# Sliding-window attention with a gated MLP: VectorE precedence for product additions in the last three blocks, in place of a hold on the second projection product in blocks 2 to 5

## Chip, cores and metric

One core of one Trainium2 chip. The metric is device time of one execution in microseconds, the median over the runs; a profiled execution gives the trace. Engines are named as in the profile: PE is TensorE, DVE is VectorE, ACT is ScalarE, POOL is GpSimd, SP is SyncE.

## What is computed

The reference runs causal attention with a window of 128 positions and an ALiBi bias (8 batches, 8 heads, 576 positions, head size 64), and passes the result through a gated MLP:

```python
scores = scale * q @ k.T;  bias = -slope[h] * |i - j|;  mask = 0 <= i - j < 128
x = softmax(where(mask, scores + bias, -1e9)) @ v         # then (4608, 512)
g = x @ w_gate                                             # w_gate, w_val: 512 x 1536
out = (g * sigmoid(g) * (x @ w_val)) @ w_out               # w_out: 1536 x 512
```

Inputs and output are 32-bit floats; the kernel computes with 16-bit operands and accumulates in PSUM in 32 bits.

## The kernel before

The 4608 tokens are nine blocks of 512 (n = 0 to 8). For each block the kernel needs x transposed (`xT`), then the hidden activations `hT` (1536 x 512, in 12 row groups m), then the projection with `w_out`. Attention for later tokens runs between the pieces of MLP work of earlier ones, until all attention is done in block 5.

**Gate and value.** In blocks 0 to 5 they are direct products: for each m one *half* is the gate (pg, L400, four matmuls of 512 columns, then tanh L418 on ScalarE and L419 on VectorE), the other the value (pv, L400, then L430 into `hT`). A block has 24 halves, counted from 0. In blocks 6 to 8 (`SEVEN_FROM = 6`) two row groups at a time, a *unit* u of 0 to 5, are computed by the seven-product scheme of Strassen (`gate_val_by_seven`, all matmuls L627): `first`, `fifth`, `second`, `sixth`, `third`, `seventh`, `fourth`. Products pile up in PSUM tiles gX, gY, gZ. VectorE adds after two of them: `third` (v1 = gY + u2, L663, then L664 into `hT`) and `seventh` (v2 = gX + p5, L670). `fourth` writes gX again, so it can't start before L670 has read gX; L679 then multiplies its SiLU by v2 into `hT`.

**Projection.** The projection of a block n >= 1 is also done by seven products (`strassen(n, t)`, matmuls L535), once for each half t of its columns, so 14 parts. Part 0 is A11 B11, part 1 (the *second projection product*) accumulates into the tile p (`p2`), part 2 is S2 T2, then S1 T1, S3 T3, S4 B22, A22 T4. VectorE makes S1 to S4 from `hT` as *sums*, for three groups c of row groups: L488 (S3), L489 (S1, in place), L490 (S2), L491 (S4). `half_plus` (L540) adds two products on VectorE for the output. The tile p2 comes from the pool `ps_a` (four banks, shared with the scores) while the gate and value of the next block are direct, and from `ps_f` afterwards. In blocks 2 to 5 the parts of the block before are spread over the halves: one part after each half whose number is in `AT = {1, 3, 4, 6, 7, 9, 11, 13, 14, 15, 17, 18, 20, 22}`, so the second products are due after halves 3 and 14. In blocks 6 to 8 one part follows every third step. The projection of block 8 is a closing stage of its own, in which both t alternate.

**Attention.** `scores` issues a group of products into `ps_a`: four banks for a wide tile (L280), two for a narrow one (L316); ScalarE takes the exponential (L286, L320) of each bank, VectorE multiplies by the mask (L292, L324). `weighted` gives av (L348).

**Order.** From step 60 on TensorE's order is that of the program text (`manual_schedule` for PE alone). The orders of VectorE and ScalarE are fixed when the program is built, by a planner that steps through its own estimate of time: whenever an engine is free it takes, of the instructions that it holds to be ready, the one that comes first in the program. Instructions issued under `tc.high_priority()` are taken ahead of all others that are ready. On the chip each engine then runs its queue in order. `later` holds sums that `ffn` issues one or two per step.

The hold that the change touches is in `ffn`: `scored[0]` is cleared before each half is handed to the driver, which may then issue attention steps; `products()` sets it. `given` counts the parts issued in the block.

Of the kernel before, what the change touches and what calls it, by code (L numbers as in the profile page):

```python
# [31 lines left out]
SEVEN_FROM = 6  # L32
# [19 lines left out]
def kernel(  # L52
# [10 lines left out]
    nc = tc.nc  # L63
# [175 lines left out]
        nc.sync.dma_start_transpose(transposed_home(name, rank), t_.rearrange("p h d -> p (h d)"))  # L239

    ex = {}
    scored = [False]

    def scores(i):

        s, p = units[i]
        def combined(n):
            return scores_128(s, (3, 7, 8)[n], 8, (s, "c", n), msk[n])

        def together(one, two):  # L250
            return [one[0] + two[0]] + one[1:] + two[1:]

        if p == 8:
            first = combined(0) if s == 0 else []
            return first + together(combined(1), combined(2))
        if p == 7 and s == 0:
            return scores_128(s, p, p, (s, p), reg[:, :, 0:P])
        if p == 7:
            return together(scores_128(s, p, p, (s, p), reg[:, :, 0:P]), combined(0))
        if p == 3:  # L260
            return scores_128(s, p, p, (s, p), reg[:, :, 0:P], i < FIRST)
        ks = (9 * s + p) % NK
        banks = []
        early_tile = i < FIRST
        e = epool.tile([P, H, 256], FP16, name="ex", tag="ex", bufs=4)
        ex[(s, p)] = e

        def products():
            scored[0] = True
            for q4 in range(2):  # L270
                two = [ps_a.tile([P, 2, 256], FP32, name="ps", tag="a") for _ in range(2)]
                banks.append(two)
                for par in range(2 if early_tile else 0):
                    o = 4 * q4 + 2 * par
                    nc.tensor.matmul(two[par], idm, bias[:, o:o + 2, :], start=True, stop=False)
                for j in range(2):
                    pair = 2 * q4 + j
                    for par in range(2):
                        rows = slice(64 * par, 64 * par + 64)
                        nc.tensor.matmul(two[par][:, j, :], kT[rows, ks, pair, :],  # L280
                                         qT[rows, p:p + 2, pair, :], start=(j == 0 and not early_tile),
                                         stop=(j == 1))

        def act(q4, par):
            o = 4 * q4 + 2 * par
            nc.scalar.activation(e[:, o:o + 2, :], banks[q4][par], AF.Exp, scale=scale)  # L286

        def mul(q4):
            if early_tile:
                return  # L290
            o = slice(4 * q4, 4 * q4 + 4)
            nc.vector.tensor_mul(e[:, o, :], e[:, o, :], reg[:, o, :])  # L292

        return [[products], [lambda: act(0, 0)], [lambda: act(0, 1), lambda: mul(0)],
                [lambda: act(1, 0)], [lambda: act(1, 1), lambda: mul(1)]]

    def scores_128(s, kt, qt, key, m, early_tile=False):

        ks = (9 * s + kt) % NK
        banks = []  # L300
        e = epool.tile([P, H, P], FP16, name="exc", tag="exc", bufs=5)
        ex[key] = e

        er4 = e.rearrange("k (a par b) q -> k a par b q", a=2, par=2)

        def products():
            scored[0] = True
            banks.extend(ps_a.tile([P, 4, P], FP32, name="psc", tag="a") for _ in range(2))
            for par in range(2 if early_tile else 0):
                nc.tensor.matmul(banks[par].rearrange("k (a b) q -> k a b q", a=2), idm,  # L310
                                 bias.rearrange("k (a par b) q -> k a par b q", a=2, par=2)
                                 [:, :, par, :, 0:P], start=True, stop=False)
            for j in range(4):
                for par in range(2):
                    rows = slice(64 * par, 64 * par + 64)
                    nc.tensor.matmul(banks[par][:, j, :], kT[rows, ks, j, :], qT[rows, qt, j, :],  # L316
                                     start=(j == 0 and not early_tile), stop=(j == 3))

        def act(par):
            nc.scalar.activation(er4[:, :, par], banks[par].rearrange("k (a b) q -> k a b q", a=2),  # L320
                                 AF.Exp, scale=scale)

        return [[products], [lambda: act(0)],
                [lambda: act(1), lambda: early_tile or nc.vector.tensor_mul(e, e, m)]]  # L324
# [182 lines left out]
    def strassen(n, t):  # L507
# [12 lines left out]
        else:  # L520
            po = ps_f.tile([P, 2, HC], FP32, name="po", tag="po", bufs=1)
            X, Y = po[:, 0, :], po[:, 1, :]
# [13 lines left out]
                                 stop=(m == HM - 1), skip_group_check=True)  # L536

        def half_plus(dst, a, b):
            with tc.high_priority() if n + 1 < SEVEN_FROM else ExitStack():
                nc.vector.scalar_tensor_tensor(out=dst, in0=a, scalar=factor, in1=b,  # L540
                                               op0=ALU.mult, op1=ALU.add)

# [72 lines left out]
    def gate_val_by_seven(n):  # L615

        x = xT[n]
        A11, A12 = x[:, 0:HK, 0:256], x[:, HK:NKB, 0:256]
        S1, A22 = x[:, 0:HK, 256:512], x[:, HK:NKB, 256:512]
        S2, S3, S4 = xsum.pop(n)  # L620
        hT[n] = hpool.tile([P, NMB, 512], FP16, name="hT", tag="hT")
        live = {}

        def product(dst, w, c0, a, start=False):
            for i in range(2):
                for kb in range(HK):
                    nc.tensor.matmul(dst[:, i, :], w[:, kb, c0 + i * P:c0 + (i + 1) * P], a[:, kb, :],  # L627
                                     start=(start and i == 0 and kb == 0),
                                     stop=(i == 1 and kb == HK - 1), skip_group_check=True)

        def first(u):
            X, Y = (ps_a.tile([P, 2, 256], FP32, name=i, tag="a", bufs=4) for i in ("gX", "gY"))
            Z = ps_f.tile([P, 2, 256], FP32, name="gZ", tag="gv")
            live[u] = X, Y, Z
            product(X, G1, 2 * u * P, A11, True)
            nc.scalar.copy(Z, X)

        def fifth(u):
            Y = live[u][1]
            product(Y, tsum[u][0], 0, S1, True)  # L640
            p5 = epool.tile([P, 2, 256], FP32, name="p5", tag="exc", bufs=5)
            nc.scalar.copy(p5, Y)
            live[u] += (p5,)

        def second(u):
            Z = live[u][2]
            product(Z, G2, 2 * u * P, A12)
            s = supool.tile([P, 2, 256], FP16, name="s1", tag="tt")
            nc.scalar.activation(s, Z, AF.Silu)
            live[u] += (s,)  # L650

        def sixth(u):
            X = live[u][0]
            product(X, tsum[u][1], 0, S2)
            u2 = epool.tile([P, 2, 256], FP32, name="u2", tag="exc", bufs=5)
            nc.scalar.copy(u2, X)
            live[u] += (u2,)

        def third(u):
            X, Y, Z, p5, u2, s = live[u][:6]  # L660
            product(Y, V2, 2 * u * P, S4)
            v_ = supool.tile([P, 2, 256], FP16, name="v1", tag="uu")
            nc.vector.tensor_add(v_, Y, u2)  # L663
            nc.vector.tensor_mul(hT[n][:, 2 * u:2 * u + 2, 0:256], s, v_)  # L664

        def seventh(u):
            X, Y, Z, p5, u2, s = live[u]
            product(X, tsum[u][2], 0, S3)
            v_ = supool.tile([P, 2, 256], FP16, name="v2", tag="uu")
            nc.vector.tensor_add(v_, X, p5)  # L670
            live[u] += (v_,)

        def fourth(u):
            X, v_ = live[u][0], live[u][-1]
            del live[u]
            product(X, tsum[u][3], 0, A22)
            s = supool.tile([P, 2, 256], FP16, name="s2", tag="tt")
            nc.scalar.activation(s, X, AF.Silu)  # L678
            nc.vector.tensor_mul(hT[n][:, 2 * u:2 * u + 2, 256:512], s, v_)  # L679

        return {f.__name__: f for f in (first, second, third, fourth, fifth, sixth, seventh)}
# [23 lines left out]
    def ffn():  # L705

        for n in range(NBLK):
# [5 lines left out]
                        yield 1.0  # L713
            if n == SEVEN_FROM:
                break
            due, given = 0, 0
            for m in range(NMB):
                for half, _ in enumerate(gate_val(n, m)):
                    scored[0] = False
                    yield 1.0  # L720
                    due += n > 1 and 2 * m + half in AT
                    while due and not (scored[0] and given % 7 == 1):
                        next(parts)
                        due, given = due - 1, given + 1
                        yield 0.75
                    if n > 1:
                        for _ in range(1 + (len(later) > 3)):
# [285 lines left out]
```

## Time and profile before

| | |
|---|---|
| median of 4 runs | 343.28 us (343.01 to 343.58) |
| profiled execution | 343.34 us, of which 341.6 us are the span of the trace |
| busy: PE, DVE, ACT, POOL | 330.1, 277.4, 207.0, 109.6 us |
| granted TensorE clock, mean over the span | 0.998 |
| chain that ended last, by engine | PE 78%, DVE 13%, ACT 5% |

The stages of the trace, from TensorE's timeline, with the busy time of PE and DVE in each:

| stage | us | PE busy | DVE busy |
|---|---|---|---|
| block 2 and start of 3 | 95.7 to 144.0 | 47.7 | 42.1 |
| blocks 3 and 4 | 144.0 to 208.0 | 64.0 | 59.8 |
| block 5 | 208.0 to 243.4 | 35.4 | 35.3 |
| block 6 and start of 7 | 243.4 to 271.4 | 28.0 | 18.6 |
| block 7 and start of 8 | 271.4 to 299.7 | 27.7 | 20.2 |
| block 8 | 299.7 to 327.5 | 27.5 | 18.6 |
| closing projection, stores | 327.5 to 341.6 | 9.5 | 6.8 |

How to read the trace's lines: a timeline line is the start, the time to the end of the last of a merged run, the engine, the line of the kernel, the operation, output<-inputs with the shape, and how many were merged; in brackets the idle time before it and what ended it. A VectorE instruction's row is longer than its place in the queue: a sum has a row of 0.42 us while the next may start 0.33 us after it, an addition from PSUM of 512 columns a row of 0.69 us and a spacing of 0.60 us. A list of waits gives the engine, line and tile that waited, what it waited for, the total in us, the number of times, and the longest.

### The profile page before, as it was taken

Reading aid. Unit: us, or ns where it says so; the run is one execution under the profiler, and the core shown is the slowest. Engines: PE = TensorE matmul, PEld = TensorE weight load, DVE = VectorE, ACT = ScalarE, POOL = GpSimd, SP = SyncE. Lnnn points to the kernel's source line nnn. Section 1 sums busy time; section 2 is a strip of 40 time slices with the busy share of each in tenths; the row PEclk is TensorE's granted clock in tenths of the full one; section 3 lists DMA queues with packets and bytes.
Section 4 is the critical chain, followed back from the end, with each engine's and each line's share of the span. In section 5 each row is a group of like instructions: output and inputs, shape, how many; then the busy total and the mean of one; then the engine's idle time right before and its main releaser. Section 6 shows DMA issues by size and latency. Waiting matters only on the chain.

```text
span 341.6 us, 7787 instructions
## 1 busy us (share of the span) xinstructions
PE 330.1 (97%) x2983; PEld 218.6 (64%) x2983; DVE 277.4 (81%) x652; ACT 207.0 (61%) x412; POOL 109.6 (32%) x136
## 2 busy tenths in 40 slices
PE   7999989999999999999999999999999999999994
PEld 4484445444456566566655655666788878888884
DVE  6577885999798779998899999999855975765683
ACT  3758676465765675666655557463477667676640
POOL 8968672649675176834017000000000000000000
PEclk9999999999999999999999999999999999999999
DMA  9999999999999999999949922041101101011014
GB/s 151 171 180 175 163 170 154 79 129 160 142 173 156 156 180 169 170 159 149 195 108 98 182 33 79 15 84 26 63 15 48 63 0 64 26 38 63 0 71 116
DMA packets 160037, 37.37 MB, mean 109 GB/s; under 512 B 147328, under 2 KB 155648, under 8 KB 160000
## 3 DMA queue, kind: packets, MB, share of 16 engines
q0 software_dynamic: 118336, 18.62, 81.4%
q1 hardware_dynamic: 40976, 17.64, 29.1%
q10 hardware_dynamic: 688, 0.62, 0.6%
q8 instruction: 23, 0.38, 0.4%
q14 instruction: 14, 0.11, 0.1%
HBM read 37.91 MB, written 9.44 MB: 139 GB/s over the span
## 4 chain that ended last, share of the span: by engine, by line
PE 78%; DVE 13%; ACT 5%; issue 2%; DMA 1%; SPq 0%; DVEq 0%
PE po L535 16%; PE pg L400 15%; PE pv L400 15%; PE gX L627 8%; PE av L348 4%; PE gY L627 4%; PE ps L280 4%; PE po L454 2%; PE p L535 2%; DVE hT L430 2%; PE gZ L627 2%; DVE uu L419 2%; ACT ex L286 2%; PE px L374 1%; ACT tt L418 1%
## 5 line engine op out<-in xcount | busy, mean ns | idle before, releaser
L400 PE MATMUL pv<-xT,wv_sb 128*128 128x512 f16 (+2 forms) x320 | 76.5, 358 | 0.6 <-DVE uu L419 0.3
L400 PE MATMUL pg<-xT,wg_sb 128*128 128x512 f16 (+2 forms) x320 | 75.8, 358 | 0.3 <-DVE xT L376 0.2
L418 ACT ACTIVATE tt<-pg 128x512 f16<-128x512 f32 (+2 forms) x70 | 41.3, 590 | 47.7 <-PE pg L400 46.6
L286 ACT ACTIVATE ex<-ps 128x512 f16<-128x512 f32 x96 | 50.0, 606 | 10.1 <-PE ps L280 10.1
L419 DVE SCALAR_TENSOR_TENSOR uu<-tt,pg 128x512 f16<-128x512 f16 (+2 forms) x69 | 45.9, 665 | 10.5 <-ACT tt L418 10.3
L430 DVE TENSOR_TENSOR hT<-uu,pv 128x512 f16<-128x512 f16 (+2 forms) x70 | 46.6, 665 | 3.0 <-PE pv L400 1.3
L185 POOL DMA_DIRECT2D va<-in_v_dram x40 | 34.4, 865 | 34.5 <-PE av L348 28.8
L400 PEld LDWEIGHTS <-wv_sb 128*128 128x128 f16 x320 | 28.3, 98 | 25.1 <-issue 3.2
L535 PEld LDWEIGHTS <-hT 128*128 128x128 f16 x384 | 37.0, 98 | 10.6 <-issue 0.8
L400 PEld LDWEIGHTS <-wg_sb 128*128 128x128 f16 x320 | 28.2, 98 | 23.3 <-issue 2.2
L191 POOL DMA_DIRECT2D kn<-in_k_dram x39 | 33.3, 857 | 20.7 <-DMA kT<-kn 11.9
L191 POOL DMA_DIRECT2D qn<-in_q_dram x39 | 33.5, 864 | 17.6 <-DMA va<-in_v_dram 9.9
L535 PEld LDWEIGHTS <-S 128*128 128x128 f16 x288 | 27.3, 98 | 8.9 <-issue 1.4
L292 DVE TENSOR_TENSOR ex<-ex,m_reg 128x1024 f16<-128x1024 f16 x42 | 28.7, 685 | 3.1 <-ACT ex L286 3.0
L351 DVE TENSOR_TENSOR x<-av,rec 128x256 f16<-128x256 f32 x72 | 28.8, 419 | 0.4
L535 PE MATMUL po<-T,S 128*128 128x256 f16 x192 | 26.5, 273 | 0.6 <-DVE S L490 0.3
L535 PE MATMUL po<-T,hT 128*128 128x256 f16 x192 | 26.0, 273 | 0.0
L679 DVE TENSOR_TENSOR hT<-s,v 128x512 f16<-128x512 f16 x18 | 7.6, 424 | 18.5 <-ACT s L678 18.5
L320 ACT ACTIVATE exc<-psc 128x512 f16<-128x512 f32 x40 | 21.3, 609 | 1.9 <-PE psc L316 1.9
L348 PEld LDWEIGHTS <-ex 128*128 128x128 f16 x384 | 17.4, 97 | 4.6 <-issue 1.2
L348 PE MATMUL av<-va,ex 128*128 128x65 f16 x384 | 19.3, 193 | 0.7 <-DMA kn<-in_k_dram 0.5
L280 PE MATMUL ps<-qT,kT 64*128 64x256 f16 x192 | 16.7, 272 | 0.4 <-DVE qT L223 0.2
(134 smaller groups left out, 536.9 us busy)
## 6 DMA issues: line engine op xcount, KB each, us to landing
out_dram<-osb SPq DMA_DIRECT2D x32, 256.0 KB, 2.5
va<-in_v_dram POOLq DMA_DIRECT2D x32, 128.0 KB, 8.2
qn<-in_q_dram POOLq DMA_DIRECT2D x31, 128.0 KB, 8.5
kn<-in_k_dram POOLq DMA_DIRECT2D x31, 128.0 KB, 8.9
wg_sb<-in_moe_w_gate_dram POOLq DMA_DIRECT2D x6, 256.0 KB, 7.6
wv_sb<-in_moe_w_val_dram POOLq DMA_DIRECT2D x6, 256.0 KB, 8.2
wo_sb<-in_moe_w_out_dram POOLq DMA_DIRECT2D x2, 768.0 KB, 8.9
kn<-in_k_dram POOLq DMA_DIRECT2D x8, 64.0 KB, 7.3
```

Source lines behind the costliest of these rows:

```text
L185: nc.gpsimd.dma_start(va[rank][p0:p1, :, 0:D], src)
L191: nc.gpsimd.dma_start(t_[p0:p1], src)
L280: nc.tensor.matmul(two[par][:, j, :], kT[rows, ks, pair, :], qT[rows, p:p + 2, pair, :], start=(j == 0 and not early_tile), stop=(j == 1))
L286: nc.scalar.activation(e[:, o:o + 2, :], banks[q4][par], AF.Exp, scale=scale)
L348: nc.tensor.matmul(av[:, j, :], w, val, start=(n == 0), stop=(n == len(todo) - 1))
L351: nc.vector.tensor_mul(x[:, 4 * half:4 * half + 4, :], av[:, :, 0:D], rec.broadcast_to([P, 4, D]))
L400: nc.tensor.matmul(ps[:, c0:c1], w[:, kb, ms], xT[n][:, kb, c0:c1], start=(kb == 0 and c0 == 0), stop=(kb == NKB - 1 and c1 == 512), skip_ ...
L418: nc.scalar.activation(tt, pg[:, c0:c1], AF.Tanh, scale=0.5)
L419: nc.vector.scalar_tensor_tensor(out=uu, in0=tt, scalar=one if (n, m) == PIN else 1.0, in1=pg[:, c0:c1], op0=ALU.add, op1=ALU.mult)
L430: nc.vector.tensor_mul(hT[n][:, m, c0:c1], acted[(n, m)][1][:, c0:c1], pv[:, c0:c1])
L535: nc.tensor.matmul(dst, a[:, m, cols], b[:, m, :], start=(start and m == 0), stop=(m == HM - 1), skip_group_check=True)
L627: nc.tensor.matmul(dst[:, i, :], w[:, kb, c0 + i * P:c0 + (i + 1) * P], a[:, kb, :], start=(start and i == 0 and kb == 0), stop=(i == 1 an ...
```

## The change

Two things are changed together. In blocks 2 to 5 the second projection product is no longer held back by one half when scores were issued since the last half: every part comes right after the half that it is due at. And VectorE's additions on the third and seventh products (L663, L670) and the `half_plus` of the projections of blocks 5 to 8, which run during blocks 6 to 8 and in the closing stage, are issued with high priority; `half_plus` of earlier projections had it already.

```diff
@@ scores, scores_128
-    scored = [False]
         def products():
-            scored[0] = True
@@ strassen
         def half_plus(dst, a, b):
-            with tc.high_priority() if n + 1 < SEVEN_FROM else ExitStack():
+            with tc.high_priority():
                 nc.vector.scalar_tensor_tensor(out=dst, in0=a, scalar=factor, in1=b,
                                                op0=ALU.mult, op1=ALU.add)
@@ gate_val_by_seven: third, seventh
-            nc.vector.tensor_add(v_, Y, u2)
+            with tc.high_priority():
+                nc.vector.tensor_add(v_, Y, u2)
...
-            nc.vector.tensor_add(v_, X, p5)
+            with tc.high_priority():
+                nc.vector.tensor_add(v_, X, p5)
@@ ffn, blocks 2 to 5
-            due, given = 0, 0
             for m in range(NMB):
                 for half, _ in enumerate(gate_val(n, m)):
-                    scored[0] = False
                     yield 1.0
-                    due += n > 1 and 2 * m + half in AT
-                    while due and not (scored[0] and given % 7 == 1):
+                    if n > 1 and 2 * m + half in AT:
                         next(parts)
-                        due, given = due - 1, given + 1
                         yield 0.75
```

More of the change, by code (lines that the diff above doesn't have):

```diff
@@ L306, in products @@
         def products():
-            scored[0] = True
             banks.extend(ps_a.tile([P, 4, P], FP32, name="psc", tag="a") for _ in range(2))
```

## Prediction

> **What bounds the kernel now.** I read the page first, then TensorE's list of waits, then the timelines at the places that the edits touch. The page's first lines, here the one on the engines:
>
> ```profile
> PE 330.1 (97%) x2983; PEld 218.6 (64%) x2983; DVE 277.4 (81%) x652; ACT 207.0 (61%) x412; POOL 109.6 (32%) x136
> ```
>
> TensorE is busy for 330.1 of 341.6 us and VectorE for 81%: TensorE's order, run without holes, is the time. So an edit counts by the TensorE waits that it makes or removes, and VectorE's order counts only where TensorE stands for it. From TensorE's list of waits (us in total, times, longest):
>
> ```profile
> PE gX L627 <- DVE v L670: 0.9, 2, 0.6
> ...
> PE po L535 <- DVE S L490: 0.3, 1, 0.3
> PE p L535 <- DVE hT L664: 0.3, 1, 0.3
> ```
>
> The first line is what precedence of the seventh product's addition (L670) can remove: two waits, 0.60 us in block 7 and 0.26 us in block 8. The third lies in the closing projection. Everything that the precedence half can win is therefore at most 0.60 + 0.26 + 0.27 = 1.13 us. The list has no line for a second projection product (L535, tile p) that waits for a bank: in blocks 2 to 5 that wait does not occur now.
>
> **The removed hold.** The hold acts only where a scores group was issued between a half of gate and value and a second projection product. I walked TensorE's timeline through blocks 2 to 5 and set each of the eight second products (100.48, 119.93, 138.75, 157.16, 177.69, 194.63, 214.10, 231.56 us) against the half at which it is due (halves 3 and 14 of its block). Seven stand at their own half. Only the one at 119.93 stands a half late: half 14 of block 2 is the pg at 117.55, scores follow, then half 15 (pv), and then the product. The timeline of all engines there:
>
> ```profile
> 118.51 0.61 PE L280 MATMUL ps<-qT,kT 64*128 64x256 f16 x8
> 118.68 0.60 ACT L418 ACTIVATE tt<-pg 128x512 f16<-128x512 f32 x1 [0.28 <-PE pg L400]
> ...
> 119.06 1.04 PE L400 MATMUL pv<-xT,wv_sb 128*128 128x512 f16 x4
> 119.17 2.06 ACT L286 ACTIVATE ex<-ps 128x512 f16<-128x512 f32 x4
> ...
> 119.93 0.82 PE L535 MATMUL p<-wo_sb,hT 128*128 128x256 f16 x6
> ```
>
> After the change these six matmuls come directly after the scores, at 119.06, ahead of pv. In these blocks their tile is of the pool ps_a, which has four buffers, and this scores group fills all four (four exponentials, L286). The product has to wait until the first exponential has left its bank. ScalarE starts that at 119.17, behind the tanh of 118.68, and one takes 606 ns: it ends at 119.78. A result reaches TensorE about 0.06 us after its end (L670: 277.00 + 0.68, TensorE goes on at 277.74), so the product starts at 119.84. **New wait: 119.84 - 119.06 = 0.78 us**, on TensorE's in-order queue, with pv of half 15, the attention's av, the third product and all that follows behind it. Now pv, 0.87 us long, covers it entirely; that cover is what goes. Nothing else moves: the second product issues six matmuls and one addition, which has precedence in these blocks already, and no DMA, so SyncE's and GpSimd's queues keep their order; the attention steps that follow are issued at the same running totals. Bounds: 0 if the later short waits take all of it up; I know of 0.32 us at 141.66 (VectorE S L490), and about 0.3 us inside the scores at 180.83 (0.92 us instead of 0.61). But the chain of waits into 141.66 comes from scores issued at 125.53, which move too, so I take nothing off; the least with both taken off is 0.16. The upper end is 1.27: ScalarE takes one more piece of an exponential's spacing, (2.06 - 0.61) / 3 = 0.49 us, ahead of the first.
>
> A wait of 0.78 us is longer than any that TensorE shows inside its stream after the start-up (0.60 us, with a granted clock of 1.00 in each stage). [...]
>
> **The precedence.** No instruction is added. 18 additions on third products (L663), 18 on seventh products (L670) and 18 of the projection (L540, those of blocks 5 to 8) go ahead of whatever else VectorE could run at that moment; sums and products into hT wait. Outside the block changes these additions already start within 0.4 us of their product, as the timeline of VectorE shows in each of the three blocks, so there I cost it at nothing; idle VectorE time of 0.6 to 2 us before each L679 is the cover. At the start of block 7 VectorE runs without a hole:
>
> ```profile
> 274.27 0.42 DVE L679 TENSOR_TENSOR hT<-s,v 128x512 f16<-128x512 f16 x1
> 274.73 0.43 DVE L489 TENSOR_TENSOR hT<-hT 128x512 f16<-128x512 f16 x1
> 275.07 0.42 DVE L551 TENSOR_SCALAR osb<-p 128x256 f32<-128x256 f32 x1
> 275.40 0.41 DVE L490 TENSOR_TENSOR S<-hT 128x512 f16<-128x512 f16 x1
> 275.74 0.68 DVE L663 TENSOR_TENSOR v<-gY,u 128x512 f16<-128x512 f32 x1
> 276.34 0.41 DVE L491 TENSOR_TENSOR S<-hT,S 128x512 f16<-128x512 f16 x1
> 276.67 0.42 DVE L664 TENSOR_TENSOR hT<-s,v 128x512 f16<-128x512 f16 x1
> 277.00 0.68 DVE L670 TENSOR_TENSOR v<-gX,p 128x512 f16<-128x512 f32 x1
> ```
>
> and TensorE's timeline beside it:
>
> ```profile
> 274.90 0.60 PE L627 MATMUL gX<-m_c,kT 128*128 128x256 f16 x4
> 275.33 0.93 PE L535 MATMUL po<-T,S 128*128 128x256 f16 x6
> ...
> 277.74 0.60 PE L627 MATMUL gX<-xT,kT 128*128 128x256 f16 x4 [0.60 <-DVE v L670]
> ```
>
> TensorE needs two results: S2 of the third pair (L490) for the fifth of the six matmuls at 275.33, and L670 for 277.74. The S2 product took 0.93 us, 0.82 elsewhere: 0.11 us of wait, so L490 is already just late (its start plus 0.48 us is when TensorE goes on: 275.33 + 4 x 0.109 + 0.11 = 275.88). L663's product ended by 274.62, so with precedence it is taken before L490, at 275.07 or 275.40. It holds VectorE for 0.60 us (275.74 to 276.34), a sum for 0.33. L490 then starts at 276.00 and TensorE goes on at 276.48 instead of 275.77: a wait of 0.71. L670 follows at 276.34, 0.66 earlier than now, and is there by 277.08; the fourth product, due at 277.03 + 0.71 = 277.74, finds it. Block 7: 0.11 + 0.60 before, 0.71 after. In block 8 the same order stands at 303.33 (L490), 303.66 (L663), 304.93 (L670): L490 moves to 303.93, TensorE goes on at 304.41 instead of 304.16, 0.25 of wait in place of 0.26. **Sum of both: -0.01 us; the wait moves from the seventh product's addition to the sum.** [...]
>
> At the end (326 to 331 us) VectorE left itself idle from 327.73 to 327.85 before L491 and did not take L663 there, so the order was made with L663 not yet ready, and precedence cannot move it before L491: the 0.27 us wait for L664 stays. The two projection additions (330.12, 330.78) already fill gaps between sums. I take 0, between -0.3 (L663 before L491) and +0.3 (the second addition before L490).
>
> What I cannot see is when the order's planner held each operation to be ready; bounds for the two block changes together are -0.86 (only L670 goes ahead, behind L490) and +1.2 (L663 and L670 both before L490, 0.60 more in each). A replay of the three blocks as lists with the trace's intervals varied, kept only where it gives VectorE's 139 operations of before in their order, put L663 alone before L490 in about 8 of 10 variations; I use it for the order only.
>
> **Sum.** On the profiled execution (343.34 us, span 341.6, 1.7 us around it): +0.78 - 0.01 + 0 = 344.11. The median of the runs is 0.06 lower: 343.28 + 0.77 = **344.05 us**.
>
> **Rivals.** (1) Not slower: the seventh's addition goes ahead of L491 and L664, but the third's does not get before L490. Both waits for L670 go, -0.86: 343.28 + 0.78 - 0.86 = 343.20. It decides if L663 counts as ready only after 275.40; for it speaks that VectorE left L663 out between 274.61 and 274.73, against it that at 270.02 it filled just such a gap. (2) Both additions before L490: 344.05 + 1.2 = 345.25. The seventh's product ends at 275.50, before L490's new turn at 276.00, which speaks for it. (3) The change does nothing: the 0.78 is taken up by the later waits and the orders stay, 343.3. (4) As (1), with the new wait taken up but 0.16: 343.28 + 0.16 - 0.86 = 342.58.
>
> **How the numbers follow.** Forecast 0.56, its own range 343.7 to 344.3; rival 1 0.16, rival 2 0.10, rival 3 0.09, rival 4 0.09. A measurement can tell about 0.2% from no change, 0.69 us: the bounds are 342.59 and 343.97. Slower: 0.52 of the forecast and rival 2, 0.62. Same: 0.04 of the forecast, 0.15 of rival 1, rival 3: 0.28. Faster: rival 4 and 0.01 of rival 1: 0.10. The range leaves out rivals 2 and 4 and reaches from just under rival 1 to above the forecast's end: 343.1 to 344.5.
>
> **What would show it.** In the changed profile: a wait of TensorE at a second product (L535, tile p) for ScalarE's ex (L286) near 119 us, 0.6 to 0.8 us; no more wait of gX for L670; in its place longer third products (po from T and S) for L490 at about 276.5 and 305. No wait near 119 would refute the first half; third products of 0.82 us at both places would mean rival 1, waits of 1.3 and 0.85 us there rival 2.

## The result, and the profile after

| | median, us | runs | lowest to highest |
|---|---|---|---|
| before | 343.15 | 60 | 342.82 to 343.70 |
| after | 343.63 | 42 | 343.21 to 345.43 |

The ratio is 1.0014 with a 95% interval of 1.0009 to 1.0018, which is +0.31 to +0.62 us; the medians differ by +0.48. The time moves up, as the forecast said, but less than the +0.77 of its sum, and by less than the 0.69 us (0.2%) set as what counts as slower.

The profiled executions of the two kernels show the same time and the same span, 343.34 and 341.6 us. That is chance: in after TensorE goes on 0.2 us earlier at 6 us, in the start-up, and the end comes 4.37 us after its last matmul starts, where it is 4.60 us in before. After's execution also lies near the low end of its runs. So the comparison below doesn't use spans. It takes the start of the same TensorE instruction in both traces and follows how the difference of the two starts changes along the stream.

| place | difference of starts, after less before, us | change |
|---|---|---|
| blocks 1 and 2, up to the scores near 118.5 us | -0.18 | |
| behind the second product of block 2 (119 us) | +0.56 | +0.74 |
| 141 us and 241 us | +0.56 | 0.00 |
| behind the fourth product of block 7 (278 us) | +0.40 | -0.16 |
| behind the fourth product of block 8 (306 us) | +0.24 | -0.16 |
| behind the last wait of the closing projection (329 us) | +0.23 | -0.01 |
| sum inside the stream | | +0.41 |

The page's line on the engines has hardly moved, so a change of this size cannot be seen there:

```profile
PE 330.0 (97%) x2983; PEld 218.8 (64%) x2983; DVE 277.4 (81%) x652; ACT 206.8 (61%) x412; POOL 109.8 (32%) x136
```

TensorE's list of waits after the change (us in total, times, longest) shows both halves. Lines of after have lower numbers: L532 was L535, L284 was L286, L487 was L490, L662 was L664.

```profile
PE po L532 <- DVE S L487: 0.9, 2, 0.5
...
PE p L532 <- ACT ex L284: 0.7, 1, 0.7
...
PE p L532 <- DVE hT L662: 0.3, 1, 0.3
```

The line for gX and VectorE's addition (0.9 us, two waits) is gone. Of the two waits of projection products for S2, one is not new: 0.32 us at 142.23 us, which is at 141.66 us in before and is the one of 0.3 us in its list. The other, 0.54 us, is in block 7. The wait for S2 in block 8 is not in the list; it shows only as a longer row (below). There is a new wait of a second product for an exponential. The wait for hT in the closing projection is where it was.

**At 119 us.** TensorE's timeline after the change:

```profile
118.33 0.61 PE L278 MATMUL ps<-qT,kT 64*128 64x256 f16 x8
119.63 0.82 PE L532 MATMUL p<-wo_sb,hT 128*128 128x256 f16 x6 [0.69 <-ACT ex L284]
120.28 1.03 PE L397 MATMUL pv<-xT,wv_sb 128*128 128x512 f16 x4
```

and ScalarE's at the same place:

```profile
118.50 0.60 ACT L415 ACTIVATE tt<-pg 128x512 f16<-128x512 f32 x1 [0.29 <-PE pg L397]
118.99 2.06 ACT L284 ACTIVATE ex<-ps 128x512 f16<-128x512 f32 x4
```

The second product stands ahead of pv now. In before, pv started 0.55 us after the scores; here the product starts 1.30 us after them, so it waited 1.30 - 0.55 = 0.75 us. It goes on 0.64 us after the first exponential's start. In the three 4 us windows from 115 to 127 us the granted clock stays at 1.00. The forecast's "nothing else moves" is not quite so: VectorE's addition of this product (L540, L537 in after) starts at 120.71 us where it was 121.49, and it and a multiplication by the mask now come ahead of a product into `hT`. TensorE loses nothing by it, since the shift stays the same up to 241 us.

**At the start of block 7.** VectorE's timeline after the change (L661 and L669 are the additions of the third and the seventh product, L487 and L488 the sums S2 and S4):

```profile
274.83 0.42 DVE L678 TENSOR_TENSOR hT<-s,v 128x512 f16<-128x512 f16 x1
275.29 0.42 DVE L486 TENSOR_TENSOR hT<-hT 128x512 f16<-128x512 f16 x1
275.63 0.42 DVE L548 TENSOR_SCALAR osb<-p 128x256 f32<-128x256 f32 x1
275.96 0.68 DVE L661 TENSOR_TENSOR v<-gY,u 128x512 f16<-128x512 f32 x1
276.56 0.42 DVE L487 TENSOR_TENSOR S<-hT 128x512 f16<-128x512 f16 x1
276.89 0.68 DVE L669 TENSOR_TENSOR v<-gX,p 128x512 f16<-128x512 f32 x1
277.49 0.42 DVE L488 TENSOR_TENSOR S<-hT,S 128x512 f16<-128x512 f16 x1
```

This is the forecast order: the third's addition ahead of S2, the seventh's ahead of S4. In block 8 it is the same. Apart from these two places and the one at 120 us, VectorE's order is that of before. TensorE beside it:

```profile
275.90 0.60 PE L532 MATMUL po<-T,S 128*128 128x256 f16 x4
277.03 0.39 PE L532 MATMUL po<-T,S 128*128 128x256 f16 x2 [0.54 <-DVE S L487]
277.26 0.60 PE L624 MATMUL gY<-xT,kT 128*128 128x256 f16 x4
277.70 0.60 PE L624 MATMUL gX<-m_reg,kT 128*128 128x256 f16 x4
278.13 0.60 PE L624 MATMUL gX<-xT,kT 128*128 128x256 f16 x4
```

The fourth product (the last line) follows the group ahead of it 0.43 us later, which is the spacing of four such matmuls when nothing is waited for (0.44). The wait is now inside the projection product: its fifth matmul starts 1.13 us after the first instead of 0.44, so 0.69 us is lost there. To the start of the group behind it (gY) the loss is 277.26 - 275.90 - 0.65 = 0.71 us, where 0.65 is the spacing of six such matmuls (303.72 to 304.37 us in before). In block 8 the projection product is one row of 1.08 us where 0.82 is usual, a wait of 0.26:

```profile
304.12 1.08 PE L532 MATMUL po<-T,S 128*128 128x256 f16 x6
```

### The profile page after: what moved, and what is told of

It reads as the page before. It is cut to its first block, busy times and chain, and to the rows that moved or that the text cites. A ratio compares the mean times of both kernels' runs of the same rounds, so it can differ in the third digit from the quotient of the medians.

```text
span 341.6 us, 7784 instructions
## 1 busy us (share of the span) xinstructions
PE 330.0 (97%) x2983; PEld 218.8 (64%) x2983; DVE 277.4 (81%) x652; ACT 206.8 (61%) x412; POOL 109.8 (32%) x136
## 4 chain that ended last, share of the span: by engine, by line
PE 75%; DVE 14%; ACT 6%; issue 2%; DMA 1%; ACTq 0%; DVEq 0%
PE po L532 16%; PE pg L397 14%; PE pv L397 14%; PE gX L624 8%; PE gY L624 4%; PE av L345 4%; PE ps L278 3%; PE p L532 2%; PE po L451 2%; DVE hT L427 2%; PE gZ L624 2%; ACT tt L415 2%; ACT ex L284 2%; DVE uu L416 2%; PE px L371 1%
## 5 line engine op out<-in xcount | busy, mean ns | idle before, releaser
L284 ACT ACTIVATE ex<-ps 128x512 f16<-128x512 f32 x96 | 50.0, 605 | 9.9 <-PE ps L278 9.9
L532 PEld LDWEIGHTS <-hT 128*128 128x128 f16 x384 | 37.0, 98 | 11.3 <-issue 1.7
L532 PEld LDWEIGHTS <-S 128*128 128x128 f16 x288 | 27.2, 98 | 9.9 <-DVE S L487 2.2
L532 PE MATMUL po<-T,S 128*128 128x256 f16 x192 | 26.8, 273 | 1.2 <-DVE S L487 0.9
L532 PE MATMUL po<-T,hT 128*128 128x256 f16 x192 | 26.0, 273 | 0.0
```

The costliest lines, as they stand in the source:

```text
L532: nc.tensor.matmul(dst, a[:, m, cols], b[:, m, :], start=(start and m == 0), stop=(m == HM - 1), skip_group_check=True)
```

## The experiments

The open questions were how much each half of the change does alone, whether the new wait at 119 us comes from the bank or from the order, and why precedence won something when a swap of equal waits was forecast. Each kernel was timed in five rounds beside before. "Shift" is the change of TensorE's starts against before, as in the table above.

| kernel | median (before beside it) | ratio, 95% interval | shift: 119 us, block 7, block 8, all |
|---|---|---|---|
| `prec_only` | 343.04 (343.25) | 0.9992, 0.9983 to 1.0001 | 0, -0.17, -0.16, -0.32 |
| `nohold_only` | 343.96 (343.25) | 1.0029, 1.0019 to 1.0039 | +0.75, 0, 0, +0.75 |
| `gv_bank` | 342.82 (343.25) | 0.9986, 0.9977 to 0.9995 | 0, -0.16, -0.16, -0.33 |
| `seventh_only` | 342.28 (343.25) | 0.9972, 0.9962 to 0.9982 | 0, -0.67, -0.42, -1.08 |
| `third_only` | 343.22 (343.21) | 1.0003, 0.9993 to 1.0013 | 0, -0.01, 0, -0.02 |
| `seventh_act` | 342.25 (343.21) | 0.9971, 0.9961 to 0.9982 | 0, -0.55, -0.42, -0.99 |

### `prec_only`: the precedence alone

The kernel before with the three precedence edits, and the hold kept.

```diff
-            with tc.high_priority() if n + 1 < SEVEN_FROM else ExitStack():
+            with tc.high_priority():
...
-            nc.vector.tensor_add(v_, Y, u2)
+            with tc.high_priority():
+                nc.vector.tensor_add(v_, Y, u2)
...
-            nc.vector.tensor_add(v_, X, p5)
+            with tc.high_priority():
+                nc.vector.tensor_add(v_, X, p5)
```

> The hold on the second projection product stays; the precedence on VectorE is as in the changed kernel. Theory (two separate terms, each read from gaps between TensorE's starts): the waits of the fourth product for the seventh's addition go (starts late by 0.76 us in block 7 and 0.42 in block 8 before), the wait inside the S2 product grows from 0.11 to 0.70 and from 0 to 0.26; sum -0.33 us, about 342.8 against 343.15, no wait of a second product for an exponential. Rival (the recorded sum): the waits swap one for one, -0.01 us, 343.15. Second rival: the two halves are not independent, and without the new wait at 119 us the precedence gives nothing.

The trace has the two steps of after, -0.17 and -0.16 us, and nothing at 119 us. Its list of TensorE's waits has no line for gX, and its line for S2 is that of after: the wait of 0.32 us that before has too, and the one in block 7.

```profile
PE po L535 <- DVE S L490: 0.9, 2, 0.5
```

By the runs alone this is inconclusive, since the interval holds 1. The trace separates it from a swap of equal waits. One of the eleven runs took 675.51 us, for a reason that is not known; the ratio is without it.

### `nohold_only`: the hold's removal alone

```diff
-                    while due and not (scored[0] and given % 7 == 1):
+                    while due:
```

> The hold is gone, the precedence is as before the change. Theory: the second product of block 2 stands right after the scores and waits 0.77 us for the first exponential to leave its bank; nothing later takes it up: +0.77 us, about 343.9 against 343.15. Rival: part of it is taken up by later short waits in blocks 2 to 5 (0.3 to 0.6 us of it), +0.2 to +0.45 us, and the precedence gives nothing.

TensorE's timeline at the place:

```profile
118.70 0.61 PE L280 MATMUL ps<-qT,kT 64*128 64x256 f16 x8
120.00 0.82 PE L535 MATMUL p<-wo_sb,hT 128*128 128x256 f16 x6 [0.69 <-ACT ex L286]
```

The product again starts 1.30 us after the scores, a wait of 0.75. The runs say +0.71. So this half alone costs more than the whole change, and the other half gives back part of it: 0.75 - 0.32 = +0.43, against +0.41 in after. The halves add up.

### `gv_bank`: the same order, another bank

The kernel after, with the second product's tile in the one block where its place changed taken from `ps_f` instead of `ps_a`. TensorE's order at 119 us is that of after.

```diff
-            p2 = (ps_f.tile([P, HC], FP32, name="p2", tag="gv") if seeded
+            p2 = (ps_f.tile([P, HC], FP32, name="p2", tag="gv") if seeded or (n, t) == (1, 1)
```

> The changed kernel, but the tile of the one second product in block 2 that follows a scores group comes from the pool of gate and value (three banks) in place of the one it shares with the scores. TensorE's order is that of the changed kernel. Theory (the wait is for a bank): the wait near 119 us goes, though the product stands right after the scores: -0.33 us against the kernel before, about 342.8. Rival (the order itself costs, value of half 15 and what follows come late): it stays at +0.45 us, about 343.6.

```profile
118.34 0.61 PE L278 MATMUL ps<-qT,kT 64*128 64x256 f16 x8
118.89 0.83 PE L532 MATMUL p<-wo_sb,hT 128*128 128x256 f16 x6
119.55 1.03 PE L397 MATMUL pv<-xT,wv_sb 128*128 128x512 f16 x4
```

The product starts 0.55 us after the scores, without a wait, although it stands directly behind them. ScalarE's first exponential starts at 119.00 here and at 118.99 in after, so ScalarE did not become faster. The wait is that for a bank of the pool which the scores have just filled. What is left of the change with that wait gone is the precedence alone: -0.33, where `prec_only` has -0.32. Here the runs show it too, with an interval clear of 1.

### `seventh_only`: precedence for the seventh's addition and nothing else

```diff
-            nc.vector.tensor_add(v_, X, p5)
+            with tc.high_priority():
+                nc.vector.tensor_add(v_, X, p5)
```

> The hold stays; only the addition on the seventh product has precedence. Theory: in VectorE's order it passes the S4 sum and the multiplication into hT in blocks 7 and 8, but not the S2 sum, which stays where it is. The wait of the fourth product falls from 0.76 to about 0.10 us in block 7 and from 0.42 to 0 in block 8, the S2 product keeps its 0.11: -1.08 us, about 342.1. Rival: something behind it is late next (the S4 sum or the multiplication into hT are needed sooner than thought) and gives back half or more: -0.5 us or less, 342.65 or more.

VectorE's timeline in block 7 (L671 is the seventh's addition here):

```profile
275.36 0.41 DVE L490 TENSOR_TENSOR S<-hT 128x512 f16<-128x512 f16 x1
275.69 0.68 DVE L663 TENSOR_TENSOR v<-gY,u 128x512 f16<-128x512 f32 x1
276.29 0.68 DVE L671 TENSOR_TENSOR v<-gX,p 128x512 f16<-128x512 f32 x1
276.89 0.41 DVE L491 TENSOR_TENSOR S<-hT,S 128x512 f16<-128x512 f16 x1
277.22 0.42 DVE L664 TENSOR_TENSOR hT<-s,v 128x512 f16<-128x512 f16 x1
```

and TensorE's:

```profile
275.29 0.93 PE L535 MATMUL po<-T,S 128*128 128x256 f16 x6
276.06 0.60 PE L627 MATMUL gY<-xT,kT 128*128 128x256 f16 x4
276.50 0.60 PE L627 MATMUL gX<-m_reg,kT 128*128 128x256 f16 x4
277.03 0.60 PE L627 MATMUL gX<-xT,kT 128*128 128x256 f16 x4
```

S2 keeps its place, so the projection product is 0.93 us long as before. The seventh's addition passes S4 and the product into hT, for which TensorE does not stand. The fourth product starts 0.53 us after the group ahead of it, where it took 1.20 before: 0.67 less. In block 8 it is 0.42 less. This is the order of rival 1, and it beats both kernels: -0.28%, with the interval clear of 1.

### `third_only`: precedence for the third's addition and nothing else

```diff
-            nc.vector.tensor_add(v_, Y, u2)
+            with tc.high_priority():
+                nc.vector.tensor_add(v_, Y, u2)
```

> The hold stays; only the addition on the third product has precedence. Theory (VectorE's order in a full stretch only passes a wait on): the addition goes ahead of the S2 sum, the S2 product of TensorE waits 0.70 us in block 7 and 0.26 in block 8 instead of 0.11 and 0, and the addition on the seventh product stays in its place, so the fourth products start at the same times as before: 0.00 us, about 343.2. Rival 1 (both waits are there, one after the other): +0.6 +0.26 = +0.85 us, 344.0. Rival 2 (the gain of the precedence is shared by its two additions): -0.16 us.

TensorE's timeline in block 7:

```profile
275.63 0.60 PE L535 MATMUL po<-T,S 128*128 128x256 f16 x4
276.76 0.39 PE L535 MATMUL po<-T,S 128*128 128x256 f16 x2 [0.53 <-DVE S L490]
276.99 0.60 PE L627 MATMUL gY<-xT,kT 128*128 128x256 f16 x4
277.43 0.60 PE L627 MATMUL gX<-m_reg,kT 128*128 128x256 f16 x4
278.03 0.60 PE L627 MATMUL gX<-xT,kT 128*128 128x256 f16 x4
```

Two waits stand here: 276.99 - 275.63 - 0.65 = 0.71 us for S2, up to the start of the group behind it, and 278.03 - 277.43 - 0.44 = 0.16 us for the seventh's addition, which has kept its place behind S4. Together 0.87; before they were 0.11 and 0.76, together 0.87. The addition's 0.60 us goes in front of S2 and the later wait shrinks by as much, so TensorE gains nothing.

### `seventh_act`: one step further

`seventh_only`, with the copy of the second product's tile (L551) on ScalarE, to free 0.34 us of VectorE ahead of S2.

```diff
-            nc.vector.tensor_scalar_mul(top[:, 0:HC], p2, factor)
+            nc.scalar.mul(top[:, 0:HC], p2, factor)
```

> As the kernel in which the seventh's addition alone has precedence (-1.08 us by TensorE's starts), and the copy of the second projection product (L551) in blocks 6 to 8 runs on ScalarE. This takes 0.33 us from VectorE in each full stretch; in VectorE's order the S4 sum then comes before the seventh's addition again. Theory: the S2 product's 0.11 us go, but the fourth product of block 7 waits about 0.3 us in place of 0.10: -0.97 us, 342.2 to 342.3, no better. Rival (VectorE's load there is what counts, not who is first): another -0.2 us, 342.0 or less.

TensorE's timeline in block 7:

```profile
275.75 0.82 PE L535 MATMUL po<-T,S 128*128 128x256 f16 x6
276.41 0.60 PE L627 MATMUL gY<-xT,kT 128*128 128x256 f16 x4
276.84 0.60 PE L627 MATMUL gX<-m_reg,kT 128*128 128x256 f16 x4
277.61 0.60 PE L627 MATMUL gX<-xT,kT 128*128 128x256 f16 x4 [0.17 <-DVE v L671]
```

The wait for S2 is gone (0.82 instead of 0.93), but VectorE's order has S4 (L491, at 276.54) ahead of the seventh's addition (276.87) again, which costs 0.33 at the fourth product. That the planner held VectorE to be free earlier is the likely reason, and not shown. Nothing is gained over `seventh_only`: the two ratios are the same within their intervals.

## Why the prediction was right, and where it was off

**The hold.** Right in mechanism, place and size: one product moves, it waits for the first exponential to free a bank of the scores' pool, forecast 0.78 us, measured 0.74 to 0.75. The 0.03 too much is the end of the exponential: the product goes on 0.64 us after its start, where 0.606 + 0.06 had been taken. That none of it would be taken up at 141.66 or 180.83 was right as well, since the shift is the same at 119, 141 and 241 us. `nohold_only` isolates the wait and `gv_bank` shows that it is the bank's.

**The clock.** The granted clock stayed at 1.00 around the new wait (115 to 127 us), and behind it the shift stays constant up to 241 us, so the wait costs its own length, 0.74 to 0.75 us, and no more. The forecast counted it so by estimate: the longest wait that it had read beside a clock of 1.00 was 0.60 us by its bracket. From start to start that wait is 0.76 us long (block 7, below), and the granted clock from 275 to 279 us is 1.00, so before already had one as long. The prediction's "granted clock of 1.00 in each stage" holds up to the end of the stream only: the closing stage of before (327.5 to 341.6 us) has 0.95. Its last matmuls end at 337.2 us, and from 340.4 to 341.5 us the granted clock is 0.50.

**The precedence.** The forecast had VectorE's order right in blocks 7 and 8, operation for operation. It had the new waits right: 0.71 and 0.25 us for S2 forecast, 0.71 and 0.26 measured. The term that was mis-sized is the waits that disappear. The step "Block 7: 0.11 + 0.60 before, 0.71 after. In block 8 ... 0.25 of wait in place of 0.26" took the 0.60 and the 0.26 from the brackets on the fourth product's line. A bracket counts from the modelled end of the matmuls ahead, whose row is 0.60 us long; without a wait, the next group starts 0.44 us after their start (276.10 to 276.54 us in before). The lines of before's TensorE timeline ahead of the fourth product of block 7, and the two in block 8:

```profile
276.54 0.60 PE L627 MATMUL gX<-m_reg,kT 128*128 128x256 f16 x4
...
304.81 0.60 PE L627 MATMUL gX<-m_reg,kT 128*128 128x256 f16 x4
305.67 0.60 PE L627 MATMUL gX<-xT,kT 128*128 128x256 f16 x4 [0.26 <-DVE v L670]
```

From start to start, in block 8 it is 305.67 - 304.81 - 0.44 = 0.42 us lost, not 0.26. In block 7 it is 277.74 - 276.54 - 0.44 = 0.76, not 0.60. The waits for S2 had been worked out from spacings, so one side of the swap was measured from start to start and the other from a bracket. With one yardstick the sum is 0.71 - (0.11 + 0.76) = -0.16 in block 7 and 0.26 - 0.42 = -0.16 in block 8: -0.32 in place of -0.01, which is what TensorE's starts show. The bound of 1.13 us on what the precedence can win was too small for the same reason: 0.76 and 0.42 alone are 1.18. `seventh_only` bears this out: -1.08 was expected of it by starts, where the brackets gave rival 1 only -0.86, and its trace shows -1.08. Its runs (-0.62 to -1.30 us) would fit both.

**VectorE's addition.** The 0.60 us for which the prediction has L663 hold VectorE is the spacing to the next operation in before (275.74 to 276.34); the row itself is 0.68 us long. In after the next operation again starts 0.60 us behind the third's addition (275.96 to 276.56), so the spacing decides, as it did in the prediction.

**The closing projection.** Forecast 0 and measured -0.01: L661 stays behind S4, and the wait for hT is 0.26 us where it was 0.27. The `half_plus` edit moves nothing: in `prec_only` VectorE's order, behind the start-up, changes only at the additions on the third and seventh products.

**The rivals.** Rival 2 (both additions ahead of S2) did not come: its waits of 1.3 and 0.85 us are not there. Rival 1's order is not that of after, but `seventh_only` shows that it was to be had. Rivals 3 and 4 needed the wait at 119 us to be taken up later, which it was not.

**The sum and the chances.** +0.74 - 0.16 - 0.16 - 0.01 = +0.41 by TensorE's starts, +0.48 by the runs, +0.77 forecast. With the waits that go read from start to start, the forecast's own figures give 0.71 - 0.87 = -0.16 and 0.25 - 0.42 = -0.17, and the sum would have been +0.78 - 0.33 = +0.45. The chances failed in a second step: the forecast's own range was 343.7 to 344.3 and the line for "slower" 343.97, near its middle, yet 0.52 of its 0.56 was put above that line. A forecast 0.08 us above a line belongs about half on each side of it.

## What to carry to other kernels

Measure every wait of TensorE from start to start, less the spacing of the same group elsewhere, and use that yardstick on both sides of a swap. In a stretch where VectorE runs without a hole, precedence for one operation delays another, and it may do no more than pass a wait on: with the third's addition alone TensorE's starts moved by 0.02 us. Give it to the one result for which TensorE stands, if what it passes is not needed soon: on the seventh's addition alone it brought 1.08 us, on both additions together 0.32. A product placed right behind a group that fills its whole PSUM pool needs other work in between, or a bank of another pool: right behind the scores it waited 0.75 us, with a bank of `ps_f` it started without a wait, and so it did in before, with pv (0.87 us) in between.

## What the runs showed of the hardware that was not expected

The bracketed idle time of a TensorE line understates what is lost. For groups of four matmuls of 256 columns it is 0.16 us short (0.60 for 0.76, 0.26 for 0.42). `third_only` has a wait of 0.16 us with no bracket at all, at 278.03.

The part ahead of the changed places scatters by several tenths from execution to execution. In after TensorE is 0.21 us ahead of before at 6 us and 0.18 ahead where block 2 begins (95.55 against 95.73 us). In `nohold_only` it is 0.19 behind at the scores (118.70 against 118.51 us), and at the start of block 7, with no shift at 119 us, 0.30 behind in `third_only` and 0.42 in `seventh_act` (274.76 and 274.88 against 274.46 us). So the spans of two single executions cannot show a difference of 0.4 us; starts inside the stream and medians of many runs can.
